# A two-layer kernel of linear attention and Mish: the first stage's products in pairs, and its key sums in one run

## The chip, the cores and the metric

The kernel runs on one core of a Trainium2 chip. A core has engines that work side by side, each through its own list of instructions in order: PE (TensorE) multiplies matrices, DVE (VectorE) and ACT (ScalarE) work on elements, POOL (GpSimd) does so too, and SP issues most DMAs. They wait for each other through semaphores. Matrix products are written to PSUM, and everything else lies in SBUF or in DRAM. The metric is the time of one execution in microseconds (us) as the device measures it, lower being better. Times of single instructions come from the trace of one profiled execution.

## The reference

Two layers, each an attention A and a dense block B with residuals around a layer norm, on x of 2048 rows and 640 columns. All four stages use the same weights in both layers. Cut to what matters here:

```python
def _A_ref(x, wqkv, w_phi, wo):          # H = 32 heads of Dh = 20
    qkv = (x @ wqkv).reshape(B, S, 3, H, Dh).transpose(2, 0, 3, 1, 4)
    q, k, v = qkv[0], qkv[1], qkv[2]
    pq = einsum("bhsd,hdf->bhsf", q, w_phi)
    pk = einsum("bhsd,hdf->bhsf", k, w_phi)
    phi_q = concatenate([softmax(pq), softmax(-pq)], axis=-1)
    phi_k = concatenate([softmax(pk), softmax(-pk)], axis=-1)
    kv = einsum("bhsf,bhsd->bhfd", phi_k, v)
    z = einsum("bhsf->bhf", phi_k)
    num = einsum("bhqf,bhfd->bhqd", phi_q, kv)
    den = einsum("bhqf,bhf->bhq", phi_q, z)[..., None] + 1e-6
    return (num / den).transpose(0, 2, 1, 3).reshape(B, S, D) @ wo

def _B_ref(x, w1, b1, w2):               # F = 1536
    h = x @ w1 + b1
    return (h * tanh(softplus(h))) @ w2

x = x + _A_ref(layernorm(x), ...);  x = x + _B_ref(layernorm(x), ...)
x = x + _A_ref(layernorm(x), ...);  x = x + _B_ref(layernorm(x), ...)
```

## The kernel before

The 2048 rows are cut into 8 blocks of 256 rows, and each block into two tiles of 128 rows, one per partition. A layer has three stages. `attend_first` runs over all blocks, makes queries, keys and values and adds up `kv` and `z`; `attend_second` divides, projects with `wo` and adds the residual; `dense` does the Mish block. The phi weights are folded into the query and key weights at the start, so that a tile's features come straight out of its product.

**Products.** `project` (L329, matmuls at L344) multiplies one tile with 640 columns of weights in two halves of 320. Every operand is held as a high and a low part in the fp32r type, and three partial products are added for each of five pieces of 128 rows: 30 matmuls of 320 columns make one product. A product stands in a PSUM tile named `mm`, of which there are two. The low parts of the rows, `xtl`, are made by DVE at L286 (`Transposed.step`) out of the rows and their high part `xth`, which ACT makes. In layer 0 the rows are turned on PE (L280) and L286 reads them from PSUM (`one`); in layer 1 they are read turned from DRAM into SBUF, and L286 reads them there (`xn`).

**Steps of a key tile.** `keys` (L406) is a generator. Its first step makes the product and copies it out of PSUM (ACT). Then `features` goes on a step at a time: two reductions and two subtractions (DVE, L368 to L371); the exponential (ACT, L374); its sums and their reciprocal (DVE, L377 and L378) and the division (POOL, L379). A `yield` of its own (L409) lets one more step pass. The last step are the sums, L414: 11 matmuls in fp32, each in two passes and so with two records, that add the tile's features times its values to the accumulators `kva` and `kvz`. They use 64 or 42 columns of PE's array, in the lower or the upper half of the accumulators' partitions.

**Queries and values.** `queries` (L419) does the same, with its first subtraction on POOL (L369), and then turns the result by blocks of 32 (DVE, L423) and writes it to DRAM in four DMAs (L427, tensor `e_d`). `values` (L431) copies its product into the tile `v` and has one step.

**The order.** For each block `attend_first` goes through six products in the order of the tuple `order` (L465). After each product `advance` (L399) moves every pending generator by one step, the newest first; then the new generator joins them. So a key tile's sums come behind the fifth product after its own. With the order k0, v0, q0, k1, v1, q1 (kind and tile) the sums of tile 0 stand behind the block's last product, and those of tile 1 behind the third product of the next block. Blocks 0, 1 and 7 have orders of their own; block 7 has no sixth product there, since the last query product is made in `rest` (L501), in halves between the stages, and the sums of its two key tiles stand together. From the third product on (`n > 2`, L489) each product is preceded by a step of turning and splitting the next block's rows. ACT's instructions keep the order of the program here (`act`, L110); elsewhere in this stage a scheduler places instructions by a timeline of its own. The second stage's PE and SP orders are written out by hand.

**Buffers.** Keys' features lie in `big` tiles (five), queries' in two tiles, one for each tile of a block, and values in two tiles `v`.

Of the kernel before, what the change touches and what calls it, by code (L numbers as in the profile page):

```python
# [24 lines left out]
BT = 2  # L25
BLK = BT * P
NB = S // BLK
NT = S // P
# [14 lines left out]
def kernel(  # L43
# [25 lines left out]
    def one_tile():  # L69
        return psum.tile([P, 512], F32, tag="one", name="one", bufs=4)  # L70

    def big_tile():
        return work.tile([P, EW], F32, tag="big", name="big", bufs=5)
# [46 lines left out]
    def v_tile():  # L120
        return work.tile([P, VW], F32, tag="v", name="v", bufs=2)
# [60 lines left out]
    def load_k_weights(kv_ws):  # L182
        for k in range(KD):
            for s in range(2):
                nc.sync.dma_start(kv_ws[k][s][:, :D].bitcast(F32), wp_d[1, s, k])
# [19 lines left out]
    def load_o_weights():  # L205
        return list(make_five(KD, lambda k: wo[k * P:(k + 1) * P, :]))[1:]
# [20 lines left out]
    def fold_phi(ws, bd, raw):  # L227

        pss = {}
        for k, c in ((0, 0), (1, 0), (2, 0), (3, 0), (0, 1), (1, 1), (2, 1), (3, 1), (4, 0), (4, 1)):  # L230
            if c == 0:
                mm = None if k % 2 else mm_tile()
                pss[k] = [one_tile(), one_tile()] if k % 2 else [mm[:, 0], mm[:, 1]]
            ps = pss[k][c]
            for t in range(3 * c, 3 * c + 3):
                r, rows = raw[t]
                nc.tensor.matmul(ps[:, (t % 3) * 120:(t % 3) * 120 + rows],
                                 r[:rows, k * P:(k + 1) * P], bd[:rows, t, :rows],
                                 start=True, stop=True)
            n0, n1 = (0, 360) if c == 0 else (360, D)  # L240
            hi, lo = ws[k][0][:, n0:n1], ws[k][1][:, n0:n1]
            nc.scalar.activation(hi, ps[:, :n1 - n0], AF.Copy)
            nc.vector.tensor_tensor(lo, ps[:, :n1 - n0], hi.bitcast(F32), op=ALU.subtract)
# [55 lines left out]
    def normed(b, xt):  # L299

        xn = [row_tile() for _ in range(BT)]
        for t in range(BT):
            act(xn[t], xt[:, t, :], AF.Identity,
                                 bias=stats[:, b, 1, t:t + 1], scale=stats[:, b, 0, t:t + 1])
        return Transposed(xn)
# [23 lines left out]
    def project(xts, t, ws, col, ps=None):  # L329

        if ps is None:
            mm = mm_tile()
            ps = [mm[:, 0], mm[:, 1], mm]
        for c in range(2):
            project_half(ps[c], xts, t, ws, col, c)
        return ps
# [18 lines left out]
    def features(ps, e, pool_sub):  # L355

        eg = e.rearrange("p (g d) -> p g d", d=DH)
        eh = e.rearrange("p (h s d) -> p s h d", s=2, d=DH)
        ec = e.rearrange("p (c h s d) -> p s c h d", c=2, s=2, d=DH)[:, 1]
        if len(ps) > 2:  # L360
            act(ec, both(ps).rearrange("p c (h d) -> p c h d", d=DH), AF.Copy)
        else:
            for c in range(2):
                act(ec[:, c], ps[c][:, :HC].rearrange("p (h d) -> p h d", d=DH), AF.Copy)
        yield
        m = work.tile([P, 2, H], F32, tag="m", name="m", bufs=2)
        for s, op in ((0, ALU.max), (1, ALU.min)):
            nc.vector.tensor_reduce(m[:, s], eh[:, 1], axis=AX.X, op=op)  # L368
        (nc.gpsimd if pool_sub else nc.vector).tensor_tensor(  # L369
            eh[:, 0], eh[:, 1], m[:, 0].unsqueeze(2).to_broadcast([P, H, DH]), op=ALU.subtract)  # L370
        nc.vector.tensor_tensor(eh[:, 1], m[:, 1].unsqueeze(2).to_broadcast([P, H, DH]), eh[:, 1],  # L371
                                op=ALU.subtract)
        yield
        act(e, e, AF.Exp)  # L374
        yield
        r = work.tile([P, 2 * H], F32, tag="r", name="r", bufs=2)
        nc.vector.tensor_reduce(r, eg, axis=AX.X, op=ALU.add)  # L377
        nc.vector.reciprocal(r, r)  # L378
        nc.gpsimd.tensor_tensor(eg, eg, r.unsqueeze(2).to_broadcast([P, 2 * H, DH]), op=ALU.mult)  # L379
        yield  # L380
# [6 lines left out]
    def attend_first(layer, x_src, first):  # L387


        def fetch_normed(b):  # L390
            if layer:
                return load_turned(n2_d[b], [row_tile] * 3)
            xt = fetch(x_src, b)
            norm_scale(b, [norm_stats(t, xt) for t in range(BT)])
            return xt
# [3 lines left out]
        def advance():  # L399
            for g in pending[::-1]:  # L400
                try:
                    next(g)
                except StopIteration:
                    pending.remove(g)

        def keys(xts, i, v):  # L406
            e = big_tile()
            yield from features(project(xts, i % BT, kv_ws, 0), e, False)
            yield  # L409
            for g in range(G):  # L410
                p, n = divmod(g, 2)
                w, m = (120, 64) if g < 10 else (80, 42)
                acc, c = (kva, 120 * p) if p < 4 else (kvz, 120 * (p - 4))
                nc.tensor.matmul(acc[64 * n:64 * n + m, c:c + w], v[:, GW * g:GW * g + m],  # L414
                                 e[:, 120 * g:120 * g + w],
                                 start=(i == 0 and p in (0, 4)), stop=(i == NT - 1),
                                 skip_group_check=True)

        def queries(xts, i, ps=None):  # L419
            e = query_tile(i)  # L420
            yield from features(project(xts, i % BT, q_ws, 0) if ps is None else ps, e, True)

            nc.vector.transpose(e, e)  # L423
            b, t = divmod(i, BT)
            dst = e_d[b].rearrange("(j f) (t q s) -> t q f j s", f=32, t=BT, s=32)
            for q in range(4):
                nc.sync.dma_start(dst[t, q], e[32 * q:32 * q + 32].rearrange("f (j s) -> f j s", s=32))  # L427
                if b == NB - 1:
                    yield
# [31 lines left out]
            q_ws = load_q_weights()  # L461
        for b in range(NB):
            xts = nxt
            order = ("k0", "v0", "q0", "k1", "v1", "q1")
            if b == 0:  # L465
                order = ("v0", "q0", "v1", "k0", "q1", "k1")
            elif b == 1:
                order = ("k0", "q0", "k1", "v0", "q1", "v1")
            elif b == NB - 1:
                order = ("k0", "k1", "v0", "v1", "q0")  # L470
            vs = [v_tile() for _ in range(BT)]
            for n, (kind, t) in enumerate(order):
                t = int(t)
                i = b * BT + t
                if b == 0 and n == 1:
                    if layer:
                        load_k_weights(kv_ws)
                if b == 0 and n == 3:
                    if layer == 0:
                        fold_phi(kv_ws, bd, raw)  # L480
                    kva, kvz = one_tile(), one_tile()
                if b == NB - 1 and n == 3:
                    loaded = {0: load(0)}
                if b + 1 < NB:
                    if n == 0:
                        xt = fetch_normed(b + 1)
                    elif n == 2:
                        nxt = xt if layer else normed(b + 1, xt)
                    elif n > 2:  # L489
                        nxt.step()  # L490
                g = {"k": lambda: keys(xts, i, vs[t]), "q": lambda: queries(xts, i),
                     "v": lambda: values(xts, i, vs[t])}[kind]()
                next(g)
                advance()
                pending.append(g)
            if b == 1:
                if layer == 0:
                    spill_qk_weights(kv_ws, q_ws)
                o_ws = load_o_weights()
# [19 lines left out]
    def load(b):  # L519

        ta, tb, tc_ = big_tile(), big_tile(), pair_tile(F32)
        for t, g0 in ((ta, 0), (tb, 5)):

            src = e_d[b][120 * g0:120 * (g0 + 4) + P]
            src = bass.AP(tensor=src.tensor, offset=src.offset, ap=[[BLK, P], [120 * BLK, 5], [1, BLK]])
            nc.sync.dma_start(t.rearrange("f (g s) -> f g s", s=BLK), src)
        nc.sync.dma_start(tc_[:80, 0], e_d[b][1200:])
        return [(ta, tb)[g // 5][:, (g % 5) * BLK:(g % 5 + 1) * BLK] for g in range(10)] + [tc_[:, 0]]
# [368 lines left out]
```

## Time and profile before

| | us |
|---|---|
| median of 3 runs | 1401.89 |
| lowest, highest run | 1401.17, 1402.03 |
| the profiled execution | 1400.33 |
| its span, first to last instruction | 1398.6 |

In the profile, a row of the timeline gives start and length in us, engine, line, operation, what is written and read, and how many records were merged. PE's lengths are modelled and overlap, so that starts are what tells how long something takes. A row of a group gives busy time, the mean of one in ns, and the engine's idle time just before, with what ended it. The window rows give, for each engine, busy time and number of instructions. Where an idle time is noted in brackets, the arrow names what ended it.

### The profile page before, as it was taken

Reading aid. Unit: us, or ns where it says so; the run is one execution under the profiler, and the core shown is the slowest. Engines: PE = TensorE matmul, PEld = TensorE weight load, DVE = VectorE, ACT = ScalarE, POOL = GpSimd, SP = SyncE. Lnnn points to the kernel's source line nnn. Section 1 sums busy time; section 2 is a strip of 40 time slices with the busy share of each in tenths; the row PEclk is TensorE's granted clock in tenths of the full one; section 3 lists DMA queues with packets and bytes.
Section 4 is the critical chain, followed back from the end, with each engine's and each line's share of the span. In section 5 each row is a group of like instructions: output and inputs, shape, how many; then the busy total and the mean of one; then the engine's idle time right before and its main releaser. Section 6 shows DMA issues by size and latency. Waiting matters only on the chain. (4 is left out here: it accounts for less than half of the span.)

```text
span 1398.6 us, 28120 instructions
## 1 busy us (share of the span) xinstructions
PE 1384.2 (99%) x11528; PEld 1367.6 (98%) x11528; DVE 1074.5 (77%) x1820; ACT 584.1 (42%) x973; POOL 442.3 (32%) x334
## 2 busy tenths in 40 slices
PE   7999999999999999999999999999999999999998
PEld 7999999999999999999999999999999999999998
DVE  5798877696698877788769887887767876767775
ACT  4444344321355454545454333332234444444443
POOL 1354444343422222222234443433352211211112
PEclk9999999999999999999999999999999999999999
DMA  8533422689733423343374333357976212333200
GB/s 319 169 79 57 75 40 39 185 237 292 254 87 95 111 75 64 91 114 95 106 273 89 71 65 69 50 109 218 288 251 208 69 26 77 95 95 95 73 24 20
DMA packets 350035, 169.57 MB, mean 121 GB/s; under 512 B 286866, under 2 KB 323458, under 8 KB 349906
## 3 DMA queue, kind: packets, MB, share of 16 engines
q1 hardware_dynamic: 349906, 167.78, 44.2%
q8 instruction: 90, 1.47, 0.4%
q14 instruction: 39, 0.32, 0.1%
HBM read 104.82 MB, written 62.91 MB: 120 GB/s over the span
## 5 line engine op out<-in xcount | busy, mean ns | idle before, releaser
L735 PE MATMUL mm<-r2h,ol 128*128 128x320 f32 x1280 | 304.7, 309 | 0.0
L719 POOL TENSOR_TENSOR ol<-big,ol 128x512 fp32r<-128x512 f32 (+1 forms) x98 | 129.8, 1325 | 484.1 <-ACT ol L718 407.8
L693 PE MATMUL one<-xtl,r1h 128*128 128x256 f32 x960 | 268.2, 279 | 0.0
L693 PE MATMUL one<-xth,r1l 128*128 128x256 f32 x960 | 268.0, 279 | 0.0
L693 PE MATMUL one<-xth,r1h 128*128 128x256 f32 x960 | 265.9, 279 | 0.0
L735 PEld LDWEIGHTS mm<-r2h,ol 128*128 128x128 f32 x1280 | 219.1, 188 | 0.0
L735 PE MATMUL mm<-r2l,ol 128*128 128x320 f32 x640 | 197.3, 309 | 0.0
L344 PE MATMUL mm<-r1h,xth 128*128 128x320 f32 x600 | 188.3, 314 | 0.0
L344 PE MATMUL mm<-r1h,xtl 128*128 128x320 f32 x600 | 185.7, 310 | 0.7 <-DVE xtl L286 0.7
L344 PE MATMUL mm<-r1l,xth 128*128 128x320 f32 x600 | 185.6, 309 | 0.0
L693 PEld LDWEIGHTS one<-xtl,r1h 128*128 128x128 f32 x960 | 180.4, 188 | 0.0
L693 PEld LDWEIGHTS one<-xth,r1l 128*128 128x128 f32 x960 | 180.4, 188 | 0.0
L693 PEld LDWEIGHTS one<-xth,r1h 128*128 128x128 f32 x960 | 179.6, 188 | 0.0
L708 DVE TENSOR_SCALAR big<-big 128x512 f32<-128x512 f32 (+1 forms) x98 | 56.4, 575 | 110.7 <-ACT big L706 110.5
L379 POOL TENSOR_TENSOR r<-r,r 128x1280 f32<-128x1280 f32 x32 | 75.8, 2367 | 142.6 <-DVE r L378 136.8
L735 PEld LDWEIGHTS mm<-r2l,ol 128*128 128x128 f32 x640 | 120.2, 188 | 0.0
L710 ACT ACTIVATE big<-big,two 128x512 f32<-128x512 f32 (+1 forms) x98 | 70.1, 715 | 116.1 <-DVE big L709 116.1
L706 ACT ACTIVATE big<-one,b1s 128x256 f32<-128x256 f32 x192 | 80.8, 467 | 90.2 <-PE one L693 89.7
L718 ACT ACTIVATE ol<-big 128x512 fp32r<-128x512 f32 (+1 forms) x98 | 61.0, 622 | 135.8 <-DVE big L717 135.7
L344 PEld LDWEIGHTS mm<-r1h,xth 128*128 128x128 f32 x600 | 112.8, 188 | 2.0
L344 PEld LDWEIGHTS mm<-r1h,xtl 128*128 128x128 f32 x600 | 112.8, 188 | 1.1 <-DVE xtl L286 1.0
L344 PEld LDWEIGHTS mm<-r1l,xth 128*128 128x128 f32 x600 | 112.8, 188 | 0.0
(129 smaller groups left out, 3158.1 us busy)
## 6 DMA issues: line engine op xcount, KB each, us to landing
e_d<-r SPq DMA_DIRECT2D x128, 160.0 KB, 4.0
big<-e_d SPq DMA_DIRECT2D x32, 640.0 KB, 6.8
x_d<-xt SPq DMA_DIRECT2D x23, 640.0 KB, 4.1
xt<-x_d SPq DMA_DIRECT2D x22, 640.0 KB, 4.4
n_d<-xn SPq DMA_DIRECT2D x176, 80.0 KB, 2.1
xt<-in_x SPq DMA_DIRECT2D x16, 640.0 KB, 5.7
xn<-x_d SPq DMA_DIRECT2D x28, 320.0 KB, 4.6
v<-n_d SPq DMA_DIRECT2D x30, 256.0 KB, 2.9
```

The costliest lines, as they stand in the source:

```text
L344: nc.tensor.matmul(ps[:, :HC], a[:, sl], r, start=(k == 0 and n == 0), stop=(k == KD - 1 and n == 2))
L379: nc.gpsimd.tensor_tensor(eg, eg, r.unsqueeze(2).to_broadcast([P, 2 * H, DH]), op=ALU.mult)
L693: nc.tensor.matmul(ph[:, j, :], l, r, start=(n == 0), stop=(n == 3 * KD - 1))
L706: exps[0] = nc.scalar.activation(part(ta, 0)[:, j - js.start], ph[:, j, :], AF.Exp, bias=b1s[:, 2 * pr + j:2 * pr + j + 1]).ins
L708: nc.vector.tensor_scalar_min(e, e, E_CAP)
L710: nc.scalar.activation(r, n, AF.Ln, bias=two)
L718: nc.scalar.activation(ah[:, js], n, AF.Copy)
L719: nc.gpsimd.tensor_tensor(al[:, js], n, ah[:, js].bitcast(F32), op=ALU.subtract)
L735: nc.tensor.matmul(pys[t][:, c, :HC], l[:, j, sl], r, start=(f == 0 and n == 0), stop=(f == KF - 1 and n == 2))
```

## The change

The order of the products in the common blocks (2 to 6) puts both keys first, then both values, then both queries. And the generator of a key tile pauses for one more step in the first tiles of these blocks (`i` is 4, 6, 8, 10 and 12; `BT` is 2 and `NT` is 16). With the new order both tiles' sums would otherwise stand behind two products that follow each other; with the pause, both stand behind the first product of the next block, the second tile's ahead of the first tile's. Nothing else is edited, and no function is new.

```diff
@@ -407,6 +407,8 @@
             e = big_tile()
             yield from features(project(xts, i % BT, kv_ws, 0), e, False)
             yield
+            if i % BT == 0 and BT < i < NT - BT:
+                yield
             for g in range(G):
                 p, n = divmod(g, 2)
                 w, m = (120, 64) if g < 10 else (80, 42)
@@ -461,7 +463,7 @@
             q_ws = load_q_weights()
         for b in range(NB):
             xts = nxt
-            order = ("k0", "v0", "q0", "k1", "v1", "q1")
+            order = ("k0", "k1", "v0", "v1", "q0", "q1")
             if b == 0:
                 order = ("v0", "q0", "v1", "k0", "q1", "k1")
             elif b == 1:
```

## The prediction

> **What bounds the kernel now.** I read the page first: its busy times, its slices and the chain that ended last.
>
> ```profile
> span 1398.6 us, 28120 instructions
> PE 1384.2 (99%) x11528; PEld 1367.6 (98%) x11528; DVE 1074.5 (77%) x1820; ACT 584.1 (42%) x973; POOL 442.3 (32%) x334
> ...
> PEclk9999999999999999999999999999999999999999
> ...
> PE 44%; DVE 0%; issue 0%; DVEq 0%
> ```
>
> The chain is made of PE alone, at a full granted clock. A busy share of 99% could still hide waits, so I asked the chain in order of time for the first stage of layer 1, and the windows for one block of each layer (layer 1 above, layer 0 below).
>
> ```profile
> 862.02 13.40 PE mm L344 x90
> 876.73 13.40 PE mm L344 x90
> ```
> ```profile
> core 0: us, PE busy (x) PEld busy (x) DVE busy (x) ACT busy (x) POOL busy (x), PEclk, DMA share, GB/s
> 816.53:845.94 29.41, 29.41 (x225) 28.80 (x224) 23.86 (x27) 10.53 (x15) 12.30 (x7) 1.00 0.38 68
> 150.68:181.14 30.46, 30.46 (x235) 29.84 (x234) 25.38 (x36) 12.15 (x18) 14.05 (x10) 1.00 0.36 66
> ```
>
> The product matmuls of L344 come 90 at a time (three products), and between two such pieces lie 876.73 - 862.02 - 13.40 = 1.31 us: one run of sums (L414), and nothing else. PE waits for nobody here, so a block's length is what its own instructions take. One product matmul takes (13.40 - 0.31) / 89 = 0.147 us from start to start (0.31 is the length of the last one, below). DVE is the next engine, with 23.9 of 29.4 us and 25.4 of 30.5 us.
>
> **The change, part by part.** In blocks 2 to 6 of each layer the sums of the first key tile go one product later and meet those of the second, so that two runs of 11 sums (22 records: each is done in two passes) become one of 22. That is 5 runs fewer in a layer, 10 in all; the order in which the changed program's instructions stand on PE shows just that, with the same matmuls otherwise. No computation is added or removed.
>
> *What a run costs, layer 1.* A run alone, and the one place where two already stand together (the stage's end):
>
> ```profile
> 816.30 0.30 PE L344 MATMUL mm<-r2h,xtl 128*128 128x320 f32 x1
> 816.53 1.38 PE L414 MATMUL one<-big,v 128*64 128x120 f32 x22
> 817.84 0.41 PE L344 MATMUL mm<-r1h,xth 128*128 128x320 f32 x1
> 818.09 0.31 PE L344 MATMUL mm<-r1l,xth 128*128 128x320 f32 x1
> ```
> ```profile
> 946.44 0.30 PE L344 MATMUL one<-r2h,xtl 128*128 128x320 f32 x1
> 946.67 2.54 PE L414 MATMUL one<-big,v 128*64 128x120 f32 x44
> 949.14 0.41 PE L344 MATMUL one<-r2h,xth 128*128 128x320 f32 x1
> 949.40 0.31 PE L344 MATMUL one<-r2l,xth 128*128 128x320 f32 x1
> ```
>
> From the last product matmul ahead of the run to the second one behind it are 818.09 - 816.30 = 1.79 us, where two pitches of 0.147 would be 0.29: a run alone costs 1.50 us. The double run costs 949.40 - 946.44 - 0.29 = 2.67 us. Joining two saves 2 x 1.50 - 2.67 = 0.33 us, and 5 pairs 1.65 us. Where it comes from: 0.23 us into the run instead of 0.147, and 0.25 us after the first product matmul behind it, are together 0.19 us for the two changes of kind; the other 0.14 us are the second run's start, since 22 records more cost 2.54 - 1.38 = 1.16 us and not the 1.31 us from a run's start to the next product.
>
> *The price's two ends.* Nothing of before shows ten such joints, so I bound them. Inside a run the pitch is regular:
>
> ```profile
> 816.69 0.89 PE L414 MATMUL one<-big,v 128*64 128x120 f32 x14
> ```
> ```profile
> L414 PE MATMUL one<-big,v 128*64 128x120 f32 (+1 forms) x704 | 43.7, 267 | 0.4 <-POOL big L379 0.4
> ```
>
> One record is 0.27 us long (modelled), and a matmul's two start together, so 14 records are six pitches: (0.89 - 0.27) / 12 = 0.052 us a record. At that pitch 20 records are 1.03 us, and the two short ones of the last group some 0.07: a joint without any restart would cost 1.10 instead of 1.16 and save 0.39 us. At the other end the second tile starts as if alone, and only the two changes of kind are saved, 0.19 us. I take 0.33, because that row is the very form that the change makes.
>
> *Layer 0.* There PE also turns the next block's rows (L280), and in before such turns follow straight behind one of the two runs.
>
> ```profile
> 163.84 0.31 PE L344 MATMUL mm<-r2h,xtl 128*128 128x320 f32 x1
> 164.07 1.38 PE L414 MATMUL one<-big,v 128*64 128x120 f32 x22
> 165.38 0.66 PE L280 MATMUL one<-ident,xn 128*128 128x128 f32 x4
> ...
> 166.03 0.31 PE L344 MATMUL mm<-r1l,xth 128*128 128x320 f32 x1
> ```
> ```profile
> 170.13 0.31 PE L344 MATMUL mm<-r1h,xtl 128*128 128x320 f32 x1
> 170.28 0.60 PE L280 MATMUL one<-ident,xn 128*128 128x128 f32 x4
> ...
> 170.86 0.31 PE L344 MATMUL mm<-r1l,xth 128*128 128x320 f32 x1
> ```
> ```profile
> 174.97 0.31 PE L344 MATMUL mm<-r1h,xtl 128*128 128x320 f32 x1
> 175.12 0.38 PE L280 MATMUL one<-ident,xn 128*128 128x128 f32 x2
> ...
> 175.49 0.31 PE L344 MATMUL mm<-r2l,xth 128*128 128x320 f32 x1
> ```
>
> Four turns alone cost 170.86 - 170.13 - 0.29 = 0.44 us, so the run in front of turns cost 2.19 - 0.29 - 0.44 = 1.46, not 1.50: the two share a change of kind. Four of the five pairs have such a run and save 1.50 + 1.46 - 2.67 = 0.29 us, the fifth 0.33: 1.49 us. The changed order also splits a group of four turns into one and three in the middle blocks. Two turns cost 175.49 - 174.97 - 0.29 = 0.23, four 0.44: 0.11 each with nothing fixed, so the split costs 0 (0.1 us a block at most, were a group's rounding all fixed cost).
>
> *What moves on the other engines.* It costs nothing as long as PE's inputs are ready, so I walked the tightest path, the second key tile in layer 1, from the start of the block's first product.
>
> ```profile
> L379 POOL TENSOR_TENSOR r<-r,r 128x1280 f32<-128x1280 f32 x3 | 7.1, 2365 | 17.2 <-DVE r L378 17.2
> ...
> L423 DVE STREAM_TRANSPOSE r<-r 128x1280 f32<-128x1280 f32 x2 | 3.0, 1502 | 0.0
> ...
> L377 DVE TENSOR_REDUCE r<-big 128x64 f32<-128x1280 f32 x2 | 3.0, 1476 | 0.0
> ...
> L116 ACT ACTIVATE big<-big 128x1280 f32<-128x1280 f32 x2 | 2.5, 1264 | 0.0
> ...
> L116 ACT ACTIVATE big<-mm 128x640 f32<-128x640 f32 x2 | 1.4, 708 | 7.6 <-PE mm L344 7.6
> ```
>
> A product is 30 x 0.147 = 4.4 us. First product 4.4, the double run 2.7, three more products: the second values end at 20.3. The exponential of this tile stands behind their copy on ACT: 20.3 + 0.7 + 1.3 = 22.3. On DVE a query's transpose (1.5) may stand ahead of the sum (1.5), then a split (0.7) and the reciprocal (0.5): 26.5. POOL then divides for 2.4 us, and a query's subtraction may be ahead of it (about 1.3): 30.2 at the latest. The sums are due one product after the next block's start, 29.1 + 4.4 = 33.5. So 3.3 us are left; without that cover every us of lateness is a us of PE. The layer-0 block has 1.5 us more on DVE, and still 1.8 us left. PSUM is freed by copies of 0.7 us that may stand behind an exponential (1.3): done 2.0 us after a product, 2.4 us before the tile is needed again. Three of the five large buffers are then in use, and the first values of a block are copied only after its sums. The first query's four writes to DRAM go behind the next block's row fetch in SP's queue, so they do not hold it up; they have two products until that query's buffer is written again, as before.
>
> *Sum.* 1.65 + 1.49 = 3.1 us. The profiled execution took 1400.33 us around its span of 1398.6; it would take 1397.2. The three runs of before have their median at 1401.89, 1.56 above it, so the median goes to 1398.8.
>
> **Rivals.** *Only the changes of kind are saved.* Each joint starts anew: 10 x 0.19 = 1.9 us, 1400.0. For it: the second tile's sums wait on a semaphore of their own. Against it: so did those of the 2.54 us row, and they did not start anew.
>
> A rule of the Trainium skill (TensorEngine Tiling (Array Packing), Key Properties) says that changing the tiling mode drains the array; with the 128-cycle drain of TensorE: Matmul & The Clock Gate (Step-by-step: what each phase is for), at 2.4 GHz, my estimate is 10 x 2 x 0.053 = 1.1 us, or 1400.8. The rows show more than that at each change, 0.08 and 0.10 us.
>
> *The gain is absorbed.* Something later that does not move with PE ends a wait; then 1401.9. The first wait behind the stage is this one:
>
> ```profile
> 955.65 1.38 PE L571 MATMUL mm<-kvb,big 120*64 120x63 f32 x40 [0.43 <-PE mm L571]
> ```
>
> It is ended through PE's own earlier result, so it moves along; the last block's order is not changed. Against it also stands the chain, PE to the end.
>
> *POOL holds DVE, and PE waits (slower).* In layer 1 a double run already waits once:
>
> ```profile
> 771.42 1.38 PE L414 MATMUL one<-big,v 128*64 128x120 f32 x22 [0.45 <-POOL big L379]
> ...
> 775.78 0.41 PE L344 MATMUL mm<-r1h,xtl 128*128 128x320 f32 x1 [0.73 <-DVE xtl L286]
> ```
> ```profile
> 768.62 2.75 POOL L379 TENSOR_TENSOR big<-big,r 128x1280 f32<-128x1280 f32 x1 [1.29 <-DVE r L378]
> ```
> ```profile
> 769.07 2.84 DVE L286 TENSOR_TENSOR xtl<-xn,xth 128x512 fp32r<-128x512 f32 x1
> ```
> ```profile
> L286 DVE TENSOR_TENSOR xtl<-one,xth 128x512 fp32r<-128x512 f32 x52 | 34.4, 670 | 2.8 <-ACT xth L116 2.5
> ```
>
> The split of L286 takes 0.67 us from PSUM, but here, from SBUF, it ended 0.54 us behind POOL's division: held for its whole length. If the adjacent keys bring this into every changed block, PE loses 0.45 us at the sums in ten blocks and 0.73 us at the split in the five of layer 1: 8.2 - 3.1 = 5.1 us slower, 1407.0. It decides from the point where lateness passes the 3.3 us above. One hold adds at most 2.4; it takes two in a row on the same path. Against it: those sums are block 0's, whose keys stand fourth and last among the products, not first.
>
> The Trainium skill (SBUF — State Buffer, Terms, the shared port pair) says that the pair is locked for a whole instruction and the loser fully blocks; the two rows agree with it, 2.84 us against 0.67.
>
> **How the numbers follow.** Chances: forecast 0.70, only the changes of kind 0.10, absorbed 0.08, POOL holds DVE 0.12. A measurement here can tell about 0.2%, 2.8 us, from no change, and 3.1 us is just over it: of the forecast's 0.70 I put 0.63 beyond it and 0.07 within. So faster 0.63; same 0.07 + 0.10 + 0.08 = 0.25; slower 0.12. The low end is the joint without restart, 10 x 0.39 = 3.9 us, and the 0.7 us by which the lowest run of before lies under the median: 1397.3. The high end takes in the second case and half of the absorbed one: 1401.2.
>
> **What would show it.** Right: in layer 1's block window 29.1 us instead of 29.41 with no wait named on L414 or L344; double runs of 2.5 us from start to next product; second-stage work of layer 0 1.5 us and of layer 1 3.1 us earlier. Wrong: an idle time released by POOL ahead of the sums, a wait on the split at a block's start, or a double run of 2.6 us and more.

## The result, and the profile after

| | median, us | lowest to highest |
|---|---|---|
| before, 12 runs beside it | 1401.17 | 1400.12 to 1403.02 |
| after, 12 runs | 1397.80 | 1396.09 to 1399.34 |

The ratio after to before is 0.9974, with a 95% interval of 0.9965 to 0.9983: 3.4 us faster. The prediction was 1398.8, or 3.1 us below its own median of before. The profiled execution of after took 1396.09 us, with a span of 1394.3.

The page of after, its busy times, clock and chain:

```profile
span 1394.3 us, 28137 instructions
PE 1380.7 (99%) x11528; PEld 1367.0 (98%) x11528; DVE 1075.5 (77%) x1820; ACT 583.3 (42%) x973; POOL 440.0 (32%) x334
...
PEclk9999999999999999999999999999999999999999
...
PE 44%; DVE 0%; issue 0%; DVEq 0%
```

The same 11528 records keep PE busy for 3.5 us less, at the same granted clock, and the chain that ended last is still PE's alone. So the work itself became shorter. The windows of one block in each layer of after, from one double run of sums to the next (layer 1 above):

```profile
803.65:832.72 29.07, 29.07 (x226) 28.77 (x225) 24.05 (x27) 10.52 (x15) 12.16 (x6) 1.00 0.39 69
153.20:183.38 30.18, 30.18 (x236) 29.84 (x235) 24.10 (x35) 12.18 (x19) 13.62 (x9) 1.00 0.38 66
```

These are 29.07 and 30.18 us, where before had 29.41 and 30.46. Two joined runs on PE's timeline of after, first in layer 1, then in layer 0 (two more lines stand ahead of the sums in the code, so L414 is L416 here):

```profile
803.41 0.31 PE L344 MATMUL mm<-r1h,xtl 128*128 128x320 f32 x1
803.65 2.54 PE L416 MATMUL one<-big,v 128*64 128x120 f32 x44
806.12 0.41 PE L344 MATMUL mm<-r1h,xth 128*128 128x320 f32 x1
806.38 0.31 PE L344 MATMUL mm<-r1l,xth 128*128 128x320 f32 x1
```
```profile
152.97 0.31 PE L344 MATMUL mm<-r1l,xth 128*128 128x320 f32 x1
153.20 2.54 PE L416 MATMUL one<-big,v 128*64 128x120 f32 x44
155.67 0.41 PE L344 MATMUL mm<-r1h,xtl 128*128 128x320 f32 x1
155.93 0.31 PE L344 MATMUL mm<-r1h,xth 128*128 128x320 f32 x1
```

Both last 2.47 us from start to next product and cost 806.38 - 803.41 - 0.29 = 2.68 and 155.93 - 152.97 - 0.29 = 2.67 us. PE waits for another engine's result at two places of layer 1's first stage, the two that waited before. They stand where block 1 passes into block 2; from there to the stage's end PE waits for no other engine, and in layer 0's first stage it waits nowhere behind the first sums:

```profile
768.84 1.38 PE L416 MATMUL one<-big,v 128*64 128x120 f32 x22 [0.35 <-POOL big L379]
...
773.20 0.41 PE L344 MATMUL mm<-r1h,xtl 128*128 128x320 f32 x1 [0.73 <-DVE xtl L286]
```

Where the span's 4.3 us went is read from the starts of the same work. On PE's timeline, the first sums and the first of the second stage in each layer, before and then after:

```profile
72.49 0.73 PE L414 MATMUL one<-big,v 128*64 128x120 f32 x10
...
273.76 0.45 PE L571 MATMUL mm<-kvb,big 120*64 120x63 f32 x8
...
756.21 1.04 PE L414 MATMUL one<-big,v 128*64 128x120 f32 x16
...
952.46 0.74 PE L571 MATMUL mm<-kvb,big 120*64 120x63 f32 x18
```
```profile
71.48 1.38 PE L416 MATMUL one<-big,v 128*64 128x120 f32 x22
...
271.25 1.38 PE L573 MATMUL mm<-kvb,big 120*64 120x63 f32 x40
...
753.72 1.38 PE L416 MATMUL one<-big,v 128*64 128x120 f32 x22
...
948.18 1.39 PE L573 MATMUL mm<-kvb,big 120*64 120x63 f32 x40
```

From first sums to second stage, layer 0 took 201.27 us and now takes 199.77: 1.50 less. Layer 1 went from 196.25 to 194.46: 1.79 less. The part between them is 482.45 before and 482.47 after, and what follows 952.46 and 948.18 has kept its length too. The other 1.0 us lies ahead of the first sums, in setup code that the change does not touch.

### The profile page after: what moved, and what is told of

Read it like the earlier page. It is cut to its first block, busy times and chain, and to the rows that moved or that the text cites. A ratio compares the mean times of both kernels' runs of the same rounds, so it can differ in the third digit from the quotient of the medians.

```text
span 1394.3 us, 28137 instructions
## 1 busy us (share of the span) xinstructions
PE 1380.7 (99%) x11528; PEld 1367.0 (98%) x11528; DVE 1075.5 (77%) x1820; ACT 583.3 (42%) x973; POOL 440.0 (32%) x334
```

## The experiments

Each was timed beside before on the same chip. The stages are the lengths just explained, from each run's one profile.

| run | median | before | ratio (95%) | stage of layer 0, 1 |
|---|---|---|---|---|
| e_order | 1401.69 | 1401.89 | 1.0001 (0.9992 to 1.0010) | 201.47, 196.41 |
| e_split | 1409.58 | 1401.89 | 1.0054 (1.0041 to 1.0067) | 205.05, 201.09 |
| e_four | 1396.97 | 1401.89 | 0.9971 (0.9961 to 0.9981) | 199.07, 194.47 |
| e_apart | 1401.96 | 1401.89 | 1.0003 (0.9995 to 1.0012) | 201.94, 196.28 |
| e_apart2 | 1409.87 | 1402.18 | 1.0051 (1.0039 to 1.0064) | 204.72, 201.13 |
| e_early | 1399.71 | 1402.18 | 0.9983 (0.9974 to 0.9992) | 199.76, 196.51 |
| e_block1 | 1400.28 | 1402.18 | 0.9987 (0.9978 to 0.9996) | 199.43, 197.87 |
| e_again | 1397.71 | 1402.18 | 0.9968 (0.9955 to 0.9980) | 199.77, 194.78 |

**e_order: the new order without the pause.** The runs then stand alone again, so this tells the order's share from the joints'. Against after:

```diff
             yield
-            if i % BT == 0 and BT < i < NT - BT:
-                yield
             for g in range(G):
```

> The new order of the products alone, without the pause: the sums of the two tiles stand behind the block's last product and behind the next block's first, so no two runs meet in blocks 2 to 6. Theory (only the number of runs counts): layer 1 as before, block 29.41 us; in layer 0 no run stands in front of turned rows any more, 0.04 us more in four blocks; in all 0 to 0.2 us slower, ratio 1.000. Rival (putting the keys side by side is what pays): about 3 us faster, 0.998, with blocks near 29.07 us although the runs stay apart.

No change, within 0.1%. PE's timeline of this run, one block's two runs and the first of the next block:

```profile
802.90 1.38 PE L414 MATMUL one<-big,v 128*64 128x120 f32 x22
808.80 1.38 PE L414 MATMUL one<-big,v 128*64 128x120 f32 x22
...
832.31 1.38 PE L414 MATMUL one<-big,v 128*64 128x120 f32 x22
```

The runs are single, and a block lasts 832.31 - 802.90 = 29.41 us, as before. The order alone, with all that it moves on DVE, ACT, POOL and SP, is worth nothing. What paid is the joint that the pause makes.

**e_split: the opposite of the change.** Before, with a tile's sums cut into runs of 6 and 5 matmuls, one product apart. The condition also takes tile 3, so there are 11 cuts in a layer, 22 in all. Against before:

```diff
             for g in range(G):
+                if g == 6 and BT < i < NT - BT:
+                    yield
                 p, n = divmod(g, 2)
```

> The opposite of the change: the kernel before, with each tile's sums of blocks 2 to 6 cut into runs of 6 and 5 matmuls that stand one product apart; 20 runs more in all. Theory (a further run costs 0.33 us, of which 0.19 for two changes of kind and 0.14 for its start): 20 x 0.33 = 6.6 us, less some 0.2 us where turned rows stand behind a run: 6.4 us slower, ratio 1.0046, layer 1's block 29.41 + 0.66 = 30.07 us. Rival (only the changes of kind cost): 20 x 0.19 = 3.8 us, 1.0027, block 29.79 us.

The windows of this run, one block of layer 1:

```profile
843.28:873.39 30.11, 30.11 (x226) 28.80 (x225) 24.30 (x28) 10.63 (x15) 12.31 (x6) 1.00 0.38 66
```

Two cuts lengthen a block from 29.41 to 30.11 us, 0.35 us each, against a joint's (29.41 - 29.07) = 0.34. The rival, 0.19 a cut, would have given 29.79. The medians say the same: 22 x 0.35 = 7.7 us, and 1409.58 - 1401.89 = 7.7. (Its profile has a further 1.0 us in layer 1's stage, a wait on POOL of 1.46 us at 777.0 where before had 0.45.) So the gain follows the number of runs, in both directions.

**e_four: twice as long runs.** The sums of blocks 2 and 3 stand in one run, and those of 4 and 5. Here the sums of blocks 2 and 4 take the values of the block behind them, so that part of the output is another; the instructions are the same in kind and number. Against after, cut:

```diff
-            if i % BT == 0 and BT < i < NT - BT:
-                yield
+            if BT < i < NT - BT:
+                for _ in range((i % BT == 0) + (6 if i // BT in (2, 4) else 0)):
+                    yield
+                if i // BT in (2, 4):
+                    v = every[i // BT + 1][i % BT]
             for g in range(G):
...
             vs = [v_tile() for _ in range(BT)]
+            every.append(vs)
```

> The change carried on: the sums of blocks 2 and 3, and of blocks 4 and 5, stand in one run of 44 matmuls; block 6 as in the change. The sums of blocks 2 and 4 read the values of the block behind them, which is not what the reference computes; the work is the same. Theory: 14 joints where the change has ten, 14 x 0.33 - 0.2 = 4.4 us faster than before, ratio 0.9969; a run of four tiles lasts 2.47 + 2 x 1.16 = 4.8 us from its start to the next product. Rival (a joint of more tiles starts anew, or PE waits for the tile that is ready last): no more than the change's 3.3 us, with idle time released by POOL on L414's matmuls.

PE's timeline of this run, a run of four tiles in layer 1:

```profile
832.33 0.31 PE L344 MATMUL mm<-r1h,xtl 128*128 128x320 f32 x1
832.57 4.87 PE L420 MATMUL one<-big,v 128*64 128x120 f32 x88
837.37 0.41 PE L344 MATMUL mm<-r1h,xth 128*128 128x320 f32 x1
837.62 0.31 PE L344 MATMUL mm<-r1l,xth 128*128 128x320 f32 x1
```

It costs 837.62 - 832.33 - 0.29 = 5.00 us, which is 2.67 + 2 x 1.165: each further tile adds what the second one added. Layer 0's stage is 0.70 us shorter than after's, the two further joints. In layer 1 they are hidden in this profile by a longer wait at 770.9 (1.06 us on POOL, in after 0.35). The median is 4.9 us below before. Its interval overlaps that of after, so the runs do not show it faster than after. A form with the right values would need more value tiles; it was not tried.

**e_apart: the same joints in another order.** The common blocks go k0, q0, k1, v0, q1, v1, and tile 0 pauses two steps, so that both sums again stand together. Against after:

```diff
             if i % BT == 0 and BT < i < NT - BT:
                 yield
+                yield
...
-            order = ("k0", "k1", "v0", "v1", "q0", "q1")
+            order = ("k0", "q0", "k1", "v0", "q1", "v1")
```

> The sums of both tiles in one run, but the keys not side by side: order k0, q0, k1, v0, q1, v1 and a pause of two steps for tile 0 in blocks 2 to 6. Theory: ten joints of 0.33 us as in the change, 3.1 us faster, ratio 0.998, layer 1's block 29.07 us, double runs of 2.47 us. Rival (the order pays): 0 us, 1.000.

The gain did not come: 1.0003. The joints are there, and a steady block of layer 1 lasts 29.07 us. But PE now waits once more in each layer, in the first product of block 3, whose rows are split during block 2, the first with this order. PE's timeline of this run, at both places:

```profile
123.98 0.41 PE L344 MATMUL mm<-r1h,xtl 128*128 128x320 f32 x1 [1.69 <-DVE xtl L286]
...
808.68 0.41 PE L344 MATMUL mm<-r1h,xtl 128*128 128x320 f32 x1 [1.11 <-DVE xtl L286]
```

The split is late. The timeline of the other engines tells why, in layer 0:

```profile
116.55 2.37 POOL L379 TENSOR_TENSOR big<-big,r 128x1280 f32<-128x1280 f32 x1
117.49 2.12 DVE L371 TENSOR_TENSOR big<-m,big 128x640 f32<-128x640 f32 x1
...
119.70 1.28 ACT L116 ACTIVATE big<-big 128x1280 f32<-128x1280 f32 x1 [3.34 <-DVE big L371]
...
120.88 0.37 ACT L116 ACTIVATE xth<-one 128x256 fp32r<-128x256 f32 x1
...
123.52 0.41 DVE L286 TENSOR_TENSOR xtl<-one,xth 128x256 fp32r<-128x256 f32 x1
```

A division on POOL (ends 118.92) meets a subtraction on DVE (L371, 0.82 us at 799.80 of this run), which lasts 2.12 us and ends 0.69 behind it. The exponential on ACT waits for that subtraction, the high part `xth` stands behind the exponential, and the split takes it only when DVE's reductions are through. In layer 1 the same split is itself held (POOL from 807.08):

```profile
807.08 1.27 POOL L369 TENSOR_TENSOR r<-r,m 128x640 f32<-128x640 f32 x1
807.32 1.31 DVE L286 TENSOR_TENSOR xtl<-xn,xth 128x256 fp32r<-128x256 f32 x1
```

The holds, 2.12 - 0.82 = 1.30 us in layer 0 and 1.31 - 0.41 = 0.90 in layer 1, are most of the two waits (1.69 and 1.11); the same split took 0.41 us from SBUF at 784.86 of e_apart2, with POOL idle. With the wait for POOL near 775, 0.81 us here and 0.35 in after, the waits make 3.3 of the 4.0 us by which the two stages are longer than after's. The rest was not traced. So the slower rival's mechanism occurs: here it came with the loss of the whole gain, and in after, where POOL also holds splits, PE does not wait for them in these blocks. No run takes the hold alone away.

**e_apart2: a smoother way into that order.** Block 1 goes k0, q0, k1, v0, v1, q1, and tile 1 pauses one step less (the entry for tile 2 changes nothing). Against e_apart, cut:

```diff
-            yield
-            if i % BT == 0 and BT < i < NT - BT:
-                yield
+            for _ in range({1: 0, 2: 1}.get(i, 1 + 2 * (i % BT == 0 and BT < i < NT - BT))):
                 yield
...
             elif b == 1:
-                order = ("k0", "q0", "k1", "v0", "q1", "v1")
+                order = ("k0", "q0", "k1", "v0", "v1", "q1")
```

> The run before had its joints (block 29.07 us in layer 1) and still no gain, because PE waited 1.7 and 1.1 us for the third split at the start of block 2. Here block 1 makes its second query last (order k0, q0, k1, v0, v1, q1, tile 1's sums a step earlier), so that one product more lies between the turned rows and their use. Theory: those two waits go, the joints stay, 3.1 us faster than before, 0.998. Rival (keys apart cost the gain in some other way): 1.000 with the waits gone.

A miss: 7.7 us slower than before. The expectation puts the two waits of e_apart at the start of block 2; by the count of products they stand in block 3's first product. They did shrink, to nothing in layer 0 and 0.19 us in layer 1, but others came and grew. The largest one in layer 1 on PE's timeline, and what DVE did ahead of it:

```profile
785.32 0.64 PE L344 MATMUL mm<-r1h,xtl 128*128 128x320 f32 x1 [2.61 <-DVE xtl L286]
```
```profile
782.06 1.51 DVE L424 STREAM_TRANSPOSE r<-r 128x1280 f32<-128x1280 f32 x1 [2.55 <-POOL r L379]
783.49 1.44 DVE L377 TENSOR_REDUCE r<-big 128x64 f32<-128x1280 f32 x1
784.86 0.41 DVE L286 TENSOR_TENSOR xtl<-xn,xth 128x256 fp32r<-128x256 f32 x1
```

Here the split is short; it stands on DVE behind a query's transpose, and that waits 2.55 us for POOL's division. In layer 0 a product waits 2.37 us (at 121.87) for PSUM, freed late by ACT's copy of block 2's second query. That copy itself waited for the DMA out of the query tile that it writes:

```profile
121.11 0.70 ACT L116 ACTIVATE r<-mm 128x640 f32<-128x640 f32 x1 [8.68 <-DMA e_d<-r]
```

The edit puts block 1's second query last, so that the next one for the same tile comes five products later instead of six. Behind both waits, 2.61 and 2.37 us, PE ran at half clock for 3.41 us, as in e_block1 below. That is 12.8 matmuls at a pitch of 0.267 us; at 0.147 they need 1.88 us, so each stretch cost about 1.5 us more.

**e_early: the other way to join.** No pause for tile 0, but one step less for the second tiles (the condition takes tile 3 of block 1 too). Against after:

```diff
-            yield
-            if i % BT == 0 and BT < i < NT - BT:
+            if not (i % BT == 1 and BT < i < NT - BT):
                 yield
```

> The change with the joint placed a product earlier: no pause for tile 0, and one step less for tile 1, so that both sums are due behind the block's last product. Tests the room that the walk left, 3.3 us in layer 1 and 1.8 us in layer 0. In the changed kernel POOL's division of tile 1 ends 5.0 us ahead of the sums in layer 1 and 3.5 us in layer 0; a product less is 4.4 us. Theory: the joints pay as before (3.1 us), PE waits at most 0.5 us a block for POOL, 0 to 3 us faster, 0.998 to 1.000; layer 1's block 29.07 us. Rival (there was no room): waits of over 1 us in each of ten blocks, over 1.005.

The joints come in all ten blocks without a wait, and layer 0's stage is after's to 0.01 us. Layer 1's is 2.05 us longer, nearly all of it in two waits where block 2 begins: 0.96 us at 772.2 (0.35 in after), and this one on PE's timeline:

```profile
783.16 1.38 PE L415 MATMUL one<-big,v 128*64 128x120 f32 x22 [1.37 <-POOL big L379]
```

That is tile 3, whose sums the edit asks for a product earlier, and which lies outside the ten blocks. Within them the earlier joints cost nothing; whether the edit without tile 3 would do as well as the change was not tried.

**e_block1: one joint more.** Tile 2 pauses three steps, to meet tile 3; what was the wait at 768.84 should go. Against after:

```diff
-            yield
-            if i % BT == 0 and BT < i < NT - BT:
+            for _ in range({2: 3}.get(i, 1 + (i % BT == 0 and BT < i < NT - BT))):
                 yield
```

> The change, and tile 2's sums put off by two steps so that block 1's two runs meet as well. Theory: one joint more in layer 0 (0.33 us); in layer 1 the double run that waits for POOL is taken apart and block 1's is made, so that the number of runs stays and the wait of 0.35 to 1.5 us ahead of the sums goes. 3.5 to 4.5 us faster than before, 0.997. Rival: the wait moves to another place (the split at block 2's start), 3.3 us as the change.

Layer 0 gains the joint: 0.34 us. In layer 1 the wait on POOL is gone, and the wait on the split behind it grew from 0.73 to 2.66 us, with 0.26 at 772.0. On the timeline of this run, PE and DVE:

```profile
775.81 0.42 PE L344 MATMUL mm<-r1h,xtl 128*128 128x320 f32 x1 [2.66 <-DVE xtl L286]
```
```profile
774.72 1.03 DVE L286 TENSOR_TENSOR xtl<-xn,xth 128x256 fp32r<-128x256 f32 x1
```

PE now reaches the split earlier, and the split did not come earlier. The four idle times differ by 0.26 + 2.66 - 0.35 - 0.73 = 1.84 us, yet the stage is 3.41 us longer. The windows behind the wait have the rest:

```profile
775.81:779.66 3.85, 3.85 (x16) 3.85 (x16) 3.85 (x4) 0.00 (x0) 2.37 (x1) 0.56 0.23 68
779.66:783.50 3.84, 3.84 (x28) 3.84 (x28) 3.84 (x6) 1.86 (x2) 2.37 (x1) 1.00 0.33 49
```

At equal length the rows count 16 matmuls in the first and 28 in the second, two of these running in across its edge. The granted clock is 0.56 in the first and 1.00 in the second: after this wait PE ran at half speed for some 3.4 us, with pitches of 0.267 instead of 0.147 us. The first 15 matmuls behind the wait took 3.85 us; in after, behind the wait of 0.73, the same 15 took 775.51 - 773.20 = 2.31. So 1.5 us more were lost, and 1.84 + 1.5 is the 3.41 us but for 0.1.

**e_again: after, once more,** with the pause written in one line and the same steps, for the 1.0 us ahead of the first sums.

> The changed kernel once more, beside the others on one chip. 3.3 us faster, 0.9976; the first sums of layer 0 near 72.5 us, where its first profile had 71.48 us against 72.49 us of before: if that 1.0 us is the start's own scatter, it does not come again.

The ratio is 0.9968, within after's interval, and the steady block of layer 1 is the same to 0.01 us:

```profile
805.27:834.34 29.07, 29.07 (x225) 28.77 (x225) 24.02 (x26) 10.53 (x15) 12.17 (x6) 1.00 0.39 69
```

Its first sums begin at 72.61 us, where the first profile of after had 71.48 and before 72.49. The 1.0 us ahead of the first sums is scatter from one execution to the next. Layer 0's stage is 199.77 again; layer 1's is 194.78, with the wait on POOL at 0.69 instead of 0.35.

## Why the prediction was right, step by step

- **PE alone sets the length.** Right: the first stages lost 1.50 + 1.79 us, and every later mark moved by their sum and the 1.0 us of the start. Nothing was absorbed.
- **The price of a joint.** Right: five joints in layer 1 were to save 1.65 us and saved 5 x 0.34 = 1.70; layer 0 lost 1.50 us against 1.49. The other 0.1 us of layer 1 is the wait on POOL, 0.35 instead of 0.45. The row that was taken as the price, the pair at the stage's end, had the very form of the new runs, and it repeated to 0.01 us. Neither end was met: no run began anew (0.19), and none went through without its 0.06 us (0.39). The rule cited from the Trainium skill (TensorEngine Tiling (Array Packing), Key Properties) priced only the changes of kind. By it the gain would have been 1.1 us; the two stages measured 3.3.
- **The split turns cost nothing.** Right: layer 0's five joints gave all that was reckoned, with the turns in one and three. In e_order, with the turns split too and no joint, layer 0's stage is 0.20 us longer than before's, where 0.16 were reckoned for runs that no longer stand in front of turns.
- **The tightest path.** Cautious for the path that was walked, but another is tighter. On POOL's timeline of after, in layer 1:

```profile
825.32 2.37 POOL L379 TENSOR_TENSOR big<-big,r 128x1280 f32<-128x1280 f32 x1 [1.42 <-DVE r L378]
827.64 1.46 POOL L369 TENSOR_TENSOR r<-r,m 128x640 f32<-128x640 f32 x1
```

The second tile's division ends at 827.69, and its sums begin at 832.72: 5.0 us are left where at least 3.3 were reckoned. The query's subtraction came behind the division, not ahead of it. In layer 0 3.5 us were left, against 1.8. The walk left out the third split of the next block's rows, which PE needs at the 15th matmul of that block's first product. On the timelines of DVE and PE, in the same block of after:

```profile
826.47 1.50 DVE L286 TENSOR_TENSOR xtl<-xn,xth 128x256 fp32r<-128x256 f32 x1
```
```profile
830.28 0.31 PE L344 MATMUL mm<-r1h,xtl 128*128 128x320 f32 x1
```

The split ends at 827.97: 2.3 us are left, less than at the sums. In before it ended at 830.66 for a matmul at 834.70, 4.0 us ahead. The longest waits of e_apart and e_block1 are on this split. That its room would do was not reckoned; there the forecast had luck.

- **The slower rival.** It did not happen here, but its mechanism is shown by e_apart. One argument against it was wrong: the sums that wait at 771.42 of before are not block 0's. e_block1 holds back tile 2 alone, and the run there vanished, so they belong to block 1's first key tile, which stands first among the products. What kept the change clear of it is the room in the point above, 5.0 us at the sums and 2.3 at the split, not the place of the keys. Both signs of being wrong, a wait for POOL ahead of sums and one on the split, stand in after only where before had them. Its price was too low as well: it had no half-speed stretch behind a long wait.
- **The size.** 1.0 us too high in the median: 0.7 of it is before's own median, 1401.17 here and 1401.89 where the prediction started, and 0.3 is gain beyond 3.1. In the profiled execution it was 1396.09 against 1397.2, by the scatter at the start and the shorter wait.

Open stays why a tile that joins a run costs 1.165 us and not the 1.10 of a regular pitch. Why the wait on POOL near 770 us differs from run to run (0.35 to 1.46 us over the kernels here) was not tried by itself.

## What to carry to other kernels

When PE never waits, count its changes between kinds of matmul: each run of narrow fp32 matmuls that disappears into another was worth 0.34 us here, and a cut cost as much. Price such an edit by a place in the trace that already has the new form, then look for the smallest margin on the engines that feed PE, since the same joints in another order gave nothing. Walk every feed, not only that of the matmuls that move: here the sums had 5.0 us to spare and the split of the next rows 2.3, and it was the split that PE waited for in e_apart and e_block1.

## What the runs showed of the hardware

- **Three waits cost more than themselves.** Behind PE's waits of 2.37 and 2.61 us (e_apart2) and 2.66 us (e_block1) came a stretch of 3.41 us at a granted clock of 0.50, in which a product matmul started every 0.267 us instead of every 0.147. Behind 1.69 us (e_apart) there was none; no run has a wait of a length between these behind the setup. In e_apart2 the stretch behind 2.37 us began only 1.1 us after PE had gone on. The Trainium skill (TensorE: Matmul & The Clock Gate, Part 1) describes such a gate, at half the clock, with a window of about 3.4 us and idle time of at least one such window before it. The stretch and the half clock agree; the idle time here was shorter.
- **POOL holds DVE.** A subtraction on DVE with both inputs in SBUF that met a tensor operation of POOL ended 0.69 us behind it and took longer: 2.12 us instead of 0.82 in the row of e_apart at 117.49. The split at 807.32 there took 1.31 us from SBUF beside POOL's subtraction; the same split from PSUM at 123.52 took 0.41, though such a subtraction ran from 123.27 to 124.54.
